# Experts' second layer of the second batch pair as a turned Strassen product

## The chip, the core and the metric

The kernel runs on one core of a Trainium2 chip. A core has engines that run their own instruction streams and wait for one another by semaphores: TensorE (PE, the matmuls, with its weight loads as PEld), VectorE (DVE), ScalarE (ACT), GpSimd (POOL) and SyncE (SP), which here issues DMA transfers. Matmul results go to PSUM, which the kernel holds as eight banks of 128 partitions x 512 numbers (fp32); everything else lies in SBUF or in DRAM. The metric is the device time of one execution, in microseconds (us). The time before is 1825.17 us, the median of three runs (1821.54 to 1825.42).

## The reference

Three stages in fp32: an attention between tokens and 32 state slots in each of 4 batches, a feed-forward layer, and a layer of 8 experts with a balanced gate P. The change is in the third.

```python
def _moe2_ref(x, w_gate, w1, w2):            # x: 2176 x 512, w1: 8 x 512 x 1024, w2: 8 x 1024 x 512
    P = np.exp(x @ w_gate - max)
    ...                                      # eight rounds of row and column scaling of P
    for e in range(E):
        h = np.maximum(x @ w1[e], 0.0)
        out += P[:, e:e + 1] * (h @ w2[e])
```

Of the 2176 rows, 2048 are the tokens of the 4 batches (512 each) and 128 the state slots.

## The kernel before

**Numbers in two parts.** An fp32 matrix is held as two fp32r parts: the high part is a cast of it (an ACT copy), the low part what is left (a subtraction). A product takes three matmuls (`mm3`, L92 to L95): high by high, high by low, low by high. So a 128x128 weight block against 512 columns is three matmuls.

**Periods of the experts' stage.** The 4 batches are worked in two pairs. For each pair (g = 0, 1), each expert e and each piece fp of 256 of its 1024 hidden rows there is one period, 64 in all: n = 0 to 31 for the first pair, n = 32 to 63 for the second. In period n the first layer of piece n is computed, and beside it the second layer of piece n - 1.

**First layer** (`products`, from L837). A Strassen form: the two batches and the two halves of the hidden rows make a 2x2 block product in 7 products of 6 matmuls (L848), 42 in place of 48. They run in three PSUM banks p1a, p1b, p1c; the results are put together by DVE adds (L856) and an ACT copy (L861). `relu_split` makes the parts of h = relu(...): hh by ACT (L828), hl by DVE (L829), for each of f = 0, 1 (half of the piece) and c = 0, 1 (batch of the pair). The forms of w1 that the products need are made in the first pair by POOL sums (L751), a cast and POOL subtractions (L754), kept in DRAM, and loaded again in the second pair (L744).

**Second layer** (`second`, L917). For each batch c and each of 4 blocks t of 128 tokens, six matmuls (two hidden halves f, three each) into one of four banks of the pool `acc`; the tokens are the rows of the result, so the gate's factor is one number for each partition, and DVE adds p times factor to the sum in SBUF (L945). That is 8 groups, 48 matmuls, in a period. In the first pair a ninth group serves the state slots, with their own first layer (`slots_rows`, `slots_turned`). The second-layer weights come from DRAM as w2r, ACT casts them (L770) and POOL makes their low part (L772).

**What sets the order.** One program order for each engine is found by a scheduler from the order in which the loop emits the pieces and from when it expects them to be ready; between engines there are only semaphores. Each PSUM bank is used again as soon as the reader of its last contents is done, so a group of matmuls waits for the eviction of the group that had its bank. The four `acc` banks go round; between two uses of one bank lie at least 18 matmuls.

Of the kernel before, what the change touches and what calls it, by code (L numbers as in the profile page):

```python
# [19 lines left out]
def attention_ffn_experts(  # L20
# [85 lines left out]
    if True:  # L106
# [5 lines left out]
        mid_ctx = ExitStack()  # L112
        mid = mid_ctx.enter_context(right("mid"))
# [526 lines left out]
        for j in range(NJ):  # L640
# [3 lines left out]
            if not more:  # L644
# [3 lines left out]
                tmp = ctx.enter_context(right("tmp", reuse_waits="tile"))  # L648
# [57 lines left out]
        moe = ctx.enter_context(left("moe", reuse_waits="tile"))  # L706
        later.append(moe)
# [4 lines left out]
        w1_raw, w1_t, w2_raw, w2_t = {}, {}, {}, {}  # L712
        dram = ctx.enter_context(tc.tile_pool(name="dram", bufs=1, space=bass.MemoryType.DRAM))
        kept = {}

        def load(n):
# [41 lines left out]
        def keep_w1(n):  # L758
# [3 lines left out]
            kept[e, fp] = [dram.tile([P, 7 * 2 * P], F32, name=f"w1{s}_{n}") for s in "hl"]  # L762
            for part, of in zip(kept[e, fp], w1_t[n]):
                nc.sync.dma_start(part, f32(of[:, 1:].rearrange("a s k c -> a (s k c)")))

        def split_w2(n):
            r = w2_raw.pop(n)
            hi = moe.tile([P, 2, DM], F32R, tag="w2h", bufs=2, name=f"w2h{n}")
            lo = moe.tile([P, 2, DM], F32R, tag="w2l", bufs=2, name=f"w2l{n}")
# [3 lines left out]
            w2_t[n] = hi, lo  # L773
# [13 lines left out]
        gm, gma, cp, cs, rs = (small[:, a:b] for a, b in ((0, 1), (1, 2), (2, 2 + E), (10, 10 + E), (18, 18 + NTT)))  # L787

# [32 lines left out]

        h_t = {}

        def relu_split(n, f, c, src, cols=S):

            hi = moe.tile([P, cols], F32R, tag=f"hh{f}{c}", bufs=1 + (c > 0), name=f"hh{n}_{f}{c}")
            lo = moe.tile([P, cols], F32R, tag=f"hl{f}{c}", bufs=1 + (c > 0), name=f"hl{n}_{f}{c}")
# [198 lines left out]
```

## Time and profile before

| what | value |
|---|---|
| median of three runs | 1825.17 us (1821.54 to 1825.42) |
| profiled execution, its own time | 1825.2 us |
| its span, first to last instruction | 1823.4 us |
| mean granted TensorE clock | 0.993 of full |
| share busy: PE, DVE, POOL, ACT | 98%, 63%, 35%, 34% |

The span has four parts: attention to about 105 us, the feed-forward layer to about 400 us, the first pair's 32 periods to about 1150 us, and the second pair's 32 periods to the end. Busy time is the time in which an engine works on an instruction. The name on the left of an arrow in a row is what is written, on the right what is read; `p` stands for the four `acc` banks. A row with "xN" covers N instructions of one kind. Matmuls are pipelined: a row gives 0.39 us for one, though the next one starts earlier.

### The profile page before, as it was taken

The numbers are of one execution on the slowest core, as the hardware profiler recorded it, in microseconds if no ns is written. First come the engines' busy times: TensorE is split into PE (matmuls) and PEld (weight loads), VectorE is DVE, ScalarE is ACT, GpSimd is POOL, SyncE is SP. The second block draws the span as 40 slices with busy tenths as digits, with TensorE's granted clock in tenths as the row PEclk, the third lists the DMA queues.
The fourth block names the chain that finished last, engine by engine and source line by source line (L and its number), as shares of the span: only waits on it lengthen the run. The fifth ranks groups of instructions, "written<-read, shape, count | busy, mean of one in ns | idle before, by whom it ended". The sixth has DMA issues, their size and how long they took to land.

```text
span 1823.4 us, 21783 instructions
## 1 busy us (share of the span) xinstructions
PE 1790.6 (98%) x8328; PEld 1477.0 (81%) x8328; DVE 1145.0 (63%) x1764; ACT 615.0 (34%) x1086; POOL 640.1 (35%) x567
## 2 busy tenths in 40 slices
PE   5899999999999999999999999999999999999999
PEld 3678888878888888888888888888888888888887
DVE  6778887556876555555655556755555555555555
ACT  6876666544332222222222222221211121122211
POOL 4356554465554444444444443211111111111110
PEclk8899999999999999999999999999999999999999
DMA  5311110005343333333333332422332233223331
GB/s 146 97 40 66 58 47 18 3 28 176 133 137 127 127 116 119 127 127 127 127 127 127 127 127 105 156 104 104 137 123 104 104 125 135 105 104 115 135 114 47
DMA packets 100684, 194.89 MB, mean 107 GB/s; under 512 B 24676, under 2 KB 57444, under 8 KB 100580
## 3 DMA queue, kind: packets, MB, share of 16 engines
q1 hardware_dynamic: 99540, 193.24, 31.2%
q8 instruction: 65, 1.06, 0.2%
q10 hardware_dynamic: 1040, 0.26, 0.1%
q14 instruction: 39, 0.32, 0.1%
HBM read 130.30 MB, written 63.18 MB: 106 GB/s over the span
## 4 chain that ended last, share of the span: by engine, by line
PE 91%; DVE 4%; ACT 2%; issue 1%; POOL 1%; DMA 0%; DVEq 0%; ACTq 0%; POOLq 0%; SPq 0%
PE p1b L848 14%; PE p L94 14%; PE p L95 14%; PE p L93 14%; PE p1a L848 10%; PE p1c L848 10%; PE p1s L900 3%; PE yps L94 2%; PE yps L93 2%; PE yps L95 2%; DVE low L186 1%; PE hps L93 1%; PE hps L95 1%; PE hps L94 1%; DVE bits L182 1%
## 5 line engine op out<-in xcount | busy, mean ns | idle before, releaser
L945 DVE SCALAR_TENSOR_TENSOR oacc<-p,pr,oacc 128x512 f32<-128x512 f32 x472 | 352.5, 747 | 196.7 <-PE p L95 188.8
L95 PE MATMUL p<-w2h,hl 128*128 128x512 f32 x1088 | 424.5, 391 | 0.0
L93 PE MATMUL p<-w2h,hh 128*128 128x512 f32 x1088 | 423.7, 389 | 0.0
L94 PE MATMUL p<-w2l,hh 128*128 128x512 f32 x1088 | 423.6, 389 | 0.0
L772 POOL TENSOR_TENSOR w2l<-w2r,w2h 128x512 fp32r<-128x512 f32 x128 | 163.9, 1301 | 601.3 <-ACT w2h L770 601.3
L754 POOL TENSOR_TENSOR w1l<-w1r,w1h 128x768 fp32r<-128x768 f32 (+1 forms) x96 | 169.8, 1795 | 250.2 <-ACT w1h L752 248.6
L828 ACT ACTIVATE hh<-p1a 128x512 fp32r<-128x512 f32 x64 | 38.3, 598 | 610.7 <-PE p1a L848 610.7
L93 PEld LDWEIGHTS p<-w2h,hh 128*128 128x128 f32 x1088 | 204.2, 188 | 42.4
L94 PEld LDWEIGHTS p<-w2l,hh 128*128 128x128 f32 x1088 | 204.2, 188 | 42.1
L95 PEld LDWEIGHTS p<-w2h,hl 128*128 128x128 f32 x1088 | 204.2, 188 | 41.4
L848 PE MATMUL p1b<-xT,w1h 128*128 128x512 f32 x768 | 237.5, 390 | 0.0
L856 DVE TENSOR_TENSOR U<-p1b,P 128x512 f32<-128x512 f32 x128 | 88.4, 691 | 196.8 <-PE p1b L848 196.8
L848 PEld LDWEIGHTS p1b<-xT,w1h 128*128 128x128 f32 x768 | 142.4, 188 | 28.0
L848 PE MATMUL p1a<-xB,w1h 128*128 128x512 f32 x512 | 158.9, 391 | 0.0
L848 PE MATMUL p1b<-xT,w1l 128*128 128x512 f32 x384 | 149.6, 390 | 0.0
L401 POOL TENSOR_TENSOR gl<-t,gh 128x512 fp32r<-128x512 f32 x64 | 86.6, 1363 | 125.9 <-ACT gh L400 124.7
L751 POOL TENSOR_TENSOR w1r<-w1r 128x256 f32<-128x256 f32 x128 | 93.7, 743 | 104.4 <-DMA w1r<-in_moe_w_dram 99.4
L828 ACT ACTIVATE hh<-P 128x512 fp32r<-128x512 f32 x64 | 40.5, 632 | 264.9 <-DVE P L856 264.9
L829 DVE SCALAR_TENSOR_TENSOR hl<-U,hh 128x512 fp32r<-128x512 f32 x128 | 122.2, 955 | 6.9 <-ACT hh L828 6.8
L848 PEld LDWEIGHTS p1a<-xB,w1h 128*128 128x128 f32 x512 | 95.8, 188 | 19.1
L856 DVE TENSOR_TENSOR U<-p1c,U 128x512 f32<-128x512 f32 x128 | 87.9, 686 | 28.7 <-PE p1c L848 28.6
L94 PE MATMUL yps<-gl,woh 128*128 128x512 f32 x256 | 100.6, 393 | 0.6 <-POOL gl L401 0.6
(199 smaller groups left out, 2933.3 us busy)
## 6 DMA issues: line engine op xcount, KB each, us to landing
w1h<-w1h SPq DMA_DIRECT2D x64, 896.0 KB, 4.3
w1l<-w1l SPq DMA_DIRECT2D x64, 896.0 KB, 5.3
w2r<-in_moe_w_dram SPq DMA_DIRECT2D x64, 512.0 KB, 4.1
w1r<-in_moe_w_dram SPq DMA_DIRECT2D x128, 128.0 KB, 4.3
raw<-in_moe_w_in_dram SPq DMA_DIRECT2D x32, 256.0 KB, 2.9
raw<-in_moe_w_out_dram SPq DMA_DIRECT2D x32, 256.0 KB, 2.6
out_dram<-oacc SPq DMA_DIRECT2D x16, 256.0 KB, 2.4
x<-in_x_dram SPq DMA_DIRECT2D x12, 256.0 KB, 4.5
```

What stands on the lines that cost most here:

```text
L93: nc.tensor.matmul(ps, whi, xhi, start=start, stop=False, **k)
L94: nc.tensor.matmul(ps, whi, xlo, start=False, stop=False, **k)
L95: nc.tensor.matmul(ps, wlo, xhi, start=False, stop=stop, **k)
L401: nc.gpsimd.tensor_tensor(out=lo, in0=g, in1=f32(hi), op=ALU.subtract)
L751: nc.gpsimd.tensor_tensor(out=r[:, out], in0=r[:, a], in1=r[:, b], op=op)
L754: nc.gpsimd.tensor_tensor(out=lo[:, c0:c1], in0=r[:, c0:c1], in1=f32(hi[:, c0:c1]), op=ALU.subtract)
L772: nc.gpsimd.tensor_tensor(out=lo[:, i], in0=r[:, i], in1=f32(hi[:, i]), op=ALU.subtract)
L828: nc.scalar.activation(hi, src, AF.Relu)
L829: nc.vector.scalar_tensor_tensor(out=lo, in0=src, scalar=0.0, in1=f32(hi), op0=ALU.max, op1=ALU.subtract)
L848: nc.tensor.matmul(t[z], w[:, slot, k, :], x[:, m, k, :], start=(first and k == i == 0), stop=(k == 1 and i == 2), skip_group_check=True,)
L856: nc.vector.tensor_tensor(out=t[name], in0=a, in1=b, op=ALU.add)
L945: nc.vector.scalar_tensor_tensor(out=o, in0=ps, scalar=w, in1=o, op0=ALU.mult, op1=ALU.add)
```

## The change

1. **Second layer of the second pair, pieces 32 to 62.** The 2x2 block product (256 hidden rows by two batches, 512 columns of the result in two halves) becomes a Strassen product of 7 products P1 to P7. The result is turned: columns of d are the partitions, and 512 tokens the free side. Each product has two halves u, each of three matmuls: 42 in place of 48. The weights stand still as 128x128 blocks of w2 or its sums; the moving side is h, or its sums T1 to T4.
2. **Sums over the pieces.** Each product keeps its own sum over the 31 pieces. P6 stays in two of the four `acc` banks for good (`IN_PLACE`); the other twelve groups of a period share the two banks left. P3, P2, P7 and P5 are added to their sums in SBUF by DVE (L1114). P1 and P4 (`BY_ACT`) have their sum copied from SBUF into the bank by ACT before the matmuls (L1102), and back by ACT after (L1112).
3. **The gate.** With tokens on the free side the factor is no longer a number for each partition. It is multiplied into h by DVE (`gated`, in place of L828 and L829), from rows that a DMA spreads over all partitions once per expert; a transpose of the gate at n = 6 makes them.
4. **Forms of h.** For each piece POOL makes the sums T3, T1, T2, T4 (`less`, L939); `form` casts seven matrices by ACT (L921) and subtracts by POOL (L922).
5. **Forms of w2.** Made in the first pair (four POOL sums, a cast, two POOL subtractions for each piece, beside what is there for the first pair's own second layer), kept in DRAM by six DMAs a period, loaded in the second pair as 1 MB (`load_w2(n, 0)`) and 768 KB (`load_w2(n - 1, 1)`, one buffer). The w2r load, its cast and its two POOL subtractions go in the second pair.
6. **The end.** Piece 63 stays as it was, but for the gate (48 matmuls, DVE adds); the seven sums are put together by 14 adds, and turned back by 32 transposes in 8 groups (L1144) and 8 ACT copies (L1145), onto which piece 63 is added.
7. **Tiles.** The tiles of the first layer's results and of h come from one ring of 18 (`k2`).

```diff
...
+        def k2(name, dtype=F32, shape=(P, S)):
+            return moe.tile(list(shape), dtype, tag="k2", bufs=18, name=name)
...
+        def sum_w2(n):
+
+            r = w2_raw[n].rearrange("p i (u d) -> p i u d", u=2)
+            r11, r12, r21, r22 = r[:, 0, 0], r[:, 1, 0], r[:, 0, 1], r[:, 1, 1]
+            for out, a, b, op in (
+                (r22, r21, r22, ALU.add), (r21, r11, r21, ALU.subtract), (r11, r22, r11, ALU.subtract),
+                (r12, r12, r11, ALU.subtract),
+            ):
+                nc.gpsimd.tensor_tensor(out=out, in0=a, in1=b, op=op)
...
+        def split_s2(n):
+
+            r = w2_raw.pop(n).rearrange("p i (u d) -> p (i u) d", u=2)
+            w2_s[n] = both = over.tile([P, 2, 4, HALF], F32R, tag="w2s", name=f"w2s{n}")
+            nc.scalar.copy(both[:, 0], r)
+            for c in (0, 2):
+                nc.gpsimd.tensor_tensor(
+                    out=both[:, 1, c:c + 2], in0=r[:, c:c + 2], in1=f32(both[:, 0, c:c + 2]), op=ALU.subtract
+                )
...
+            one = dram.tile([P, 2, 4, HALF], F32, name=f"w2a_{n}")
+            two = dram.tile([P, 2, 3, HALF], F32, name=f"w2c_{n}")
+            for z in range(2):
+                nc.sync.dma_start(one[:, z, :2], b[:, z, 0::2])
+                nc.sync.dma_start(two[:, z, :2], s[:, z, 0::3])
+            nc.sync.dma_start(one[:, :, 2:], s[:, :, 1:3])
+            nc.sync.dma_start(two[:, :, 2], b[:, :, 3])
+            kept_w2[e, fp] = [one, two]
+        def load_w2(n, i):
+
+            of = kept_w2[periods[n][1:]]
+            if i < len(of):
+                slots = of[i].shape[2]
+                w2_t[n, i] = (over if i else moe).tile(
+                    [P, 2, slots, HALF], F32R, tag="w2s" if i else "w2", bufs=1 if i else 2, name=f"w2{n}_{i}"
+                )
+                nc.sync.dma_start(f32(w2_t[n, i]), of[i])
...
+        def gated(n, f, c, src, to):
+
+            e = periods[n][1]
+            rows = gate_rows["all"][:, e % 2, c].rearrange("p t q -> p (t q)")
+            nc.vector.scalar_tensor_tensor(out=to, in0=src, scalar=0.0, in1=rows, op0=ALU.max, op1=ALU.mult)
+            raw_t[n, f, c] = to
+
+        def form(n, name, raw):
+
+            hi, lo = (k2(f"{name}{s}{n}", F32R) for s in "hl")
+            nc.scalar.copy(hi, raw)
+            nc.gpsimd.tensor_tensor(out=lo, in0=raw, in1=f32(hi), op=ALU.subtract)
+            form_t[n, name] = hi, lo
...
+            gated(n, f, c, src, own)
+            if n == END:
+                form(n, f"h{f}{c}", own)
+                h_t[n, f, c] = form_t[n, f"h{f}{c}"]
+            elif (f, c) != (0, 1):
+                form(n, f"h{f}{c}", own)
...
+        def less(out, a, b):
+            nc.gpsimd.tensor_tensor(out=out, in0=a, in1=b, op=ALU.subtract)
+
+        def h_sums(n):
+
+
+            b11, b12, b21, b22 = (raw_t[n, f, c] for f in range(2) for c in range(2))
+            t3 = t2_raw[0][:, 0]
+            return [
+                lambda: less(t3, b22, b12),
+                lambda: (form(n, "T3", t3), less(b12, b12, b11)),
+                lambda: (form(n, "T1", b12), less(b22, b22, b12)),
+                lambda: (form(n, "T2", b22), less(b21, b21, b22)),
+                lambda: form(n, "T4", b21),
+            ]
...
+            if g:
+                nc.vector.tensor_tensor(out=o, in0=ps, in1=o, op=ALU.add)
...
+        ORDER = (
+            ("P3", 0, 3, "h11"), ("P1", 0, 0, "h00"), ("P2", 0, 1, "h10"), ("P7", 0, 2, "T3"),
+            ("P5", 1, 1, "T1"), ("P6", 1, 0, "T2"), ("P4", 1, 2, "T4"),
+        )
+        FIRST = len(periods) // 2
+        IN_PLACE = ("P6",)
+        BY_ACT = ("P1", "P4")
...
+                if name in IN_PLACE:
+                    held[name] = [acc_bank(f"m{name}_{i}") for i in range(2)]
...
+        def turned_product(n, name, part, slot, what, u):
+
+            w = w2_t[n, part][:, :, slot, u * P:(u + 1) * P]
+            hi, lo = form_t[n, what]
+            m = sums_of(name, u)
+            kept, first, last = name in IN_PLACE, n == FIRST, n == END - 1
+            onto = name in BY_ACT and not first
+            ps = m if kept else acc_bank(f"p2_{n}_{name}{u}")
+            if onto:
+                nc.scalar.copy(ps, m)
+            goes_on = onto or (kept and not first)
+            for i, (a, b) in enumerate(((0, hi), (1, hi), (0, lo))):
+                nc.tensor.matmul(
+                    ps, w[:, a], b, start=(i == 0 and not goes_on), stop=(i == 2 and (last or not kept)),
+                    skip_group_check=True,
+                )
+            if kept:
+                return
+            if onto or first:
+                nc.scalar.copy(m, ps)
+            else:
+                nc.vector.tensor_tensor(out=m, in0=ps, in1=m, op=ALU.add)
...
+                [lambda u=u: add(u, "P2", "P1", "P2", nc.gpsimd) for u in range(2)],
+                [lambda u=u: add(u, "P1", "P6", "P1") for u in range(2)],
+                [lambda u=u: add(u, "P5", "P1", "P5") for u in range(2)],
+                [lambda u=u: add(u, "P3", "P5", "P3", nc.gpsimd if u else nc.vector) for u in range(2)],
+                [lambda u=u: add(u, "P1", "P1", "P7", nc.gpsimd if u else nc.vector) for u in range(2)],
+                [lambda u=u: add(u, "P7", "P5", "P7", nc.gpsimd if u else nc.vector) for u in range(2)],
+                [lambda u=u: add(u, "P4", "P1", "P4") for u in range(2)],
...
+            for k in range(KD):
+                of = held[(("P2", "P4"), ("P3", "P7"))[c][k // 2]][k % 2]
+                nc.tensor.transpose(ps[:, k * P:(k + 1) * P], of[:, t * P:(t + 1) * P], ident)
+            nc.scalar.copy(oacc[1, c][:, t, :], ps)
...
+            elif n and n <= END:
+                seconds = [
+                    lambda r=r: [turned_product(n - 1, *r, u) for u in range(2)] for r in ORDER
+                ]
...
+                        load_w2(n, 0)
+                        if n > FIRST:
+                            load_w2(n - 1, 1)
...
+            if g and n < END:
+                sums_now = h_sums(n)
+                sums_now.pop(0)()
...
+        for c in (1, 0):
+            for t in range(NT):
+                turn(c, t)
+        for c in (1, 0):
+            for t in range(NT):
+                second(END, c, t)
...
```

In a steady period of the second pair TensorE has 84 matmuls in place of 90. Its order at the last product of piece 44: P40 and P41 are the two halves of product P4, p2_45_P30 and P31 the first product of the next piece. A row is one matmul, `[waits ...]` the engines it waits for (Activation is ACT). After:

```order
L1105 MATMUL p2_44_P40_13271<-T4h44_13210,w244_1_13134 128x512 [waits Activation_49]
L1105 MATMUL p2_44_P40_13271<-T4h44_13210,w244_1_13134 128x512
L1105 MATMUL p2_44_P40_13271<-T4l44_13211,w244_1_13134 128x512 [waits Pool_49]
L1105 MATMUL p2_45_P30_13304<-h11h45_13206,w245_0_13132 128x512 [waits DMAHW4_49,Activation_49]
L1105 MATMUL p2_45_P30_13304<-h11h45_13206,w245_0_13132 128x512
L1105 MATMUL p2_45_P30_13304<-h11l45_13207,w245_0_13132 128x512
L1105 MATMUL p2_44_P41_13277<-T4h44_13210,w244_1_13134 128x512 [waits Activation_49]
L1105 MATMUL p2_44_P41_13277<-T4h44_13210,w244_1_13134 128x512
L1105 MATMUL p2_44_P41_13277<-T4l44_13211,w244_1_13134 128x512
L1105 MATMUL p2_45_P31_13309<-h11h45_13206,w245_0_13132 128x512 [waits DVE_49]
```

What moved: P3 of the next piece follows P4 at once. P30 is written into the bank of P40, and its wait for Activation is for the copy of P40 out of that bank; P31 is written into the bank of P30, once DVE has read it, with the three matmuls of P41 between. Before, at the same place of the program (the second layer of piece 46, batch 1, blocks t = 0 and 1), TensorE has:

```order
L93 MATMUL p2_46_1_0_12766<-w2h46_12543,hh46_01_12655 128x512 [waits DVE_49]
L94 MATMUL p2_46_1_0_12766<-w2l46_12544,hh46_01_12655 128x512
L95 MATMUL p2_46_1_0_12766<-w2h46_12543,hl46_01_12656 128x512
L93 MATMUL p2_46_1_0_12766<-w2h46_12543,hh46_11_12599 128x512
L94 MATMUL p2_46_1_0_12766<-w2l46_12544,hh46_11_12599 128x512
L95 MATMUL p2_46_1_0_12766<-w2h46_12543,hl46_11_12600 128x512
L93 MATMUL p2_46_1_1_12785<-w2h46_12543,hh46_01_12655 128x512 [waits DVE_49]
```

What was there: six matmuls go to a bank, and the next one waits for the read of a bank filled four groups ago. ScalarE at the same place, after (T1h, T2h are casts of h's sums; m6 is the sum of P4, m2 that of P1):

```order
L921 CAST T1h45_13322<-U2_45_13152 128x512 [waits PE_49,Pool_49]
L1102 COPY p2_44_P40_13271<-m6_11250 128x512 [waits DVE_49]
L921 CAST T2h45_13349<-U3_45_13202 128x512 [waits PE_49,Pool_49]
L1112 COPY m6_11250<-p2_44_P40_13271 128x512 [waits PE_49,Activation_49]
L1102 COPY p2_44_P41_13277<-m6_11250 128x512 [waits DVE_49]
L1112 COPY m6_11250<-p2_44_P41_13277 128x512 [waits PE_49,Activation_49]
L1102 COPY p2_45_P10_13331<-m2_11140 128x512 [waits Activation_49]
L1102 COPY p2_45_P11_13337<-m2_11140 128x512 [waits DVE_49]
```

And before, where one period of the second pair has six ACT instructions, all of the first layer or of w2:

```order
L770 CAST w2h46_12543<-w2r46_12396 128x1024 [waits DMAHW3_49,PE_49,Pool_49]
L861 COPY P1_46_12539<-p1a_46_12530 128x512 [waits DVE_49,PE_49]
L828 ACTIVATE hh46_00_12617<-p1a_46_12530 128x512 [waits PE_49]
L828 ACTIVATE hh46_11_12599<-U3_46_12596 128x512 [waits DVE_49]
L828 ACTIVATE hh46_10_12636<-P1_46_12539 128x512 [waits DVE_49]
L828 ACTIVATE hh46_01_12655<-U2_46_12562 128x512 [waits DVE_49]
L770 CAST w2h47_12688<-w2r47_12541 128x1024 [waits DMAHW6_49,PE_49,Pool_49]
```

What moved: copies into and out of the product's bank stand on ACT in turn with the casts of T1 and T2, where before ACT did no work on the `acc` banks. At the end of the program, TensorE's rows after, from P5 of piece 62 on (p2_63_1_0 is the first group of piece 63):

```order
L1105 MATMUL p2_62_P50_16263<-T1h62_16186,w262_1_16166 128x512 [waits DVE_49]
L1105 MATMUL p2_62_P50_16263<-T1h62_16186,w262_1_16166 128x512
L1105 MATMUL p2_62_P50_16263<-T1l62_16187,w262_1_16166 128x512
L1105 MATMUL p2_62_P51_16268<-T1h62_16186,w262_1_16166 128x512 [waits DVE_49]
L1105 MATMUL p2_62_P51_16268<-T1h62_16186,w262_1_16166 128x512
L1105 MATMUL p2_62_P51_16268<-T1l62_16187,w262_1_16166 128x512
L1105 MATMUL p2_62_P40_16303<-T4h62_16238,w262_1_16166 128x512 [waits Activation_49]
L1105 MATMUL p2_62_P40_16303<-T4h62_16238,w262_1_16166 128x512
L1105 MATMUL p2_62_P40_16303<-T4l62_16239,w262_1_16166 128x512 [waits Pool_49]
L93 MATMUL p2_63_1_0_16379<-w263_0_16164,h01h63_16299 128x512 [waits DMAHW0_49,DVE_49]
L94 MATMUL p2_63_1_0_16379<-w263_0_16164,h01h63_16299 128x512
L95 MATMUL p2_63_1_0_16379<-w263_0_16164,h01l63_16300 128x512 [waits Pool_49]
```

What moved: piece 63 follows P4 of piece 62 in the same two banks, and no first-layer matmuls stand between these groups any more.

## Rows read from the trace of the kernel before

**Rows 1.** The page: busy time, share of the span and instructions by engine.

```profile
PE 1790.6 (98%) x8328; PEld 1477.0 (81%) x8328; DVE 1145.0 (63%) x1764; ACT 615.0 (34%) x1086; POOL 640.1 (35%) x567
```

**Rows 2.** The page: chain that ended last, by engine.

```profile
PE 91%; DVE 4%; ACT 2%; issue 1%; POOL 1%; DMA 0%; DVEq 0%; ACTq 0%; POOLq 0%; SPq 0%
```

**Rows 3.** Stretches: start:end, length, busy time by engine, clock, DMA share, GB/s.

```profile
1399.81:1420.21 20.40, 20.40 (x92) 16.89 (x90) 11.40 (x18) 4.03 (x7) 2.54 (x2) 1.00 0.32 116
1268.00:1798.00 530.00, 530.00 (x2340) 438.87 (x2339) 296.53 (x442) 104.63 (x156) 65.91 (x52) 1.00 0.31 112
600.00:624.90 24.90, 24.90 (x118) 20.79 (x117) 14.04 (x20) 6.38 (x9) 12.00 (x12) 1.00 0.39 132
90.00:105.00 15.00, 14.41 (x88) 10.37 (x86) 8.41 (x19) 10.36 (x24) 4.65 (x4) 1.00 0.01 2
```

**Rows 4.** Chain of waits from 1780 us to the end: by line; last piece.

```profile
by line: PE p L95 20.7%; PE p L93 20.6%; PE p L94 20.6%; PE p1b L848 12.4%; PE p1c L848 9.3%; PE p1a L848 6.7%; DVE oacc L945 1.7%; issue 0.1%
...
1819.57 0.75 DVE oacc L945
```

**Rows 5.** Timeline (start, length, engine): last matmul of a bank, ACT's copy.

```profile
1401.62 0.39 PE L848 MATMUL p1a<-xB,w1l 128*128 128x512 f32 x1
...
1402.05 0.59 ACT L861 COPY P<-p1a 128x512 f32<-128x512 f32 x1 [0.26 <-PE p1a L848]
```

**Rows 6.** Timeline: last matmul of a bank, DVE's add, ACT's activation.

```profile
1418.62 0.39 PE L848 MATMUL p1c<-xB,w1l 128*128 128x512 f32 x1
...
1419.05 0.69 DVE L856 TENSOR_TENSOR U<-p1c,U 128x512 f32<-128x512 f32 x1 [0.67 <-PE p1c L848]
...
1419.77 0.63 ACT L828 ACTIVATE hh<-U 128x512 fp32r<-128x512 f32 x1 [0.73 <-DVE U L856]
```

**Rows 7.** Timeline: TensorE starts again after waiting.

```profile
124.84 1.29 DVE L386 TENSOR_TENSOR t<-hps,t 128x512 f32<-128x512 f32 x2
...
125.58 0.50 PE L93 MATMUL hps<-ath,mh 128*128 128x512 f32 x1 [0.45 <-DVE t L386]
...
125.92 0.39 PE L94 MATMUL hps<-atl,mh 128*128 128x512 f32 x1
```

**Rows 8.** Answer on L423 and L408: ns min/median/max, first and last start.

```profile
L423 ACT COPY yacc<-yps x28: 559/586/596, 141.1 to 401.5; 128x512 f32<-128x512 f32 x28
...
L408 ACT COPY yps<-yacc x28: 572/590/643, 126.9 to 390.8; 128x512 f32<-128x512 f32 x28
```

**Rows 9.** The page's costliest groups: busy, mean ns, idle before.

```profile
L945 DVE SCALAR_TENSOR_TENSOR oacc<-p,pr,oacc 128x512 f32<-128x512 f32 x472 | 352.5, 747 | 196.7 <-PE p L95 188.8
...
L772 POOL TENSOR_TENSOR w2l<-w2r,w2h 128x512 fp32r<-128x512 f32 x128 | 163.9, 1301 | 601.3 <-ACT w2h L770 601.3
...
L856 DVE TENSOR_TENSOR U<-p1b,P 128x512 f32<-128x512 f32 x128 | 88.4, 691 | 196.8 <-PE p1b L848 196.8
...
L751 POOL TENSOR_TENSOR w1r<-w1r 128x256 f32<-128x256 f32 x128 | 93.7, 743 | 104.4 <-DMA w1r<-in_moe_w_dram 99.4
```

**Rows 10.** Timeline of one period of the first pair: POOL and DVE.

```profile
909.58 0.68 DVE L829 SCALAR_TENSOR_TENSOR hl<-U,hh 128x512 fp32r<-128x512 f32 x1
...
917.07 5.35 POOL L754 TENSOR_TENSOR w1l<-w1r,w1h 128x768 fp32r<-128x768 f32 x3 [9.61 <-ACT w1h L752]
917.55 1.91 DVE L829 SCALAR_TENSOR_TENSOR hl<-U,hh 128x512 fp32r<-128x512 f32 x1 [0.18 <-ACT hh L828]
```

**Rows 11.** Timeline: a group of transposes.

```profile
108.64 0.60 PE L358 MATMUL xsps<-ident,yacc_s 128*128 128x128 f32 x4
```

**Rows 12.** DMA issues from 1268 to 1798 us: KB each, us to landing.

```profile
w1h<-w1h SPq DMA_DIRECT2D x25, 896.0 KB, 4.5
w1l<-w1l SPq DMA_DIRECT2D x25, 896.0 KB, 6.4
w2r<-in_moe_w_dram SPq DMA_DIRECT2D x25, 512.0 KB, 3.3
```

More of the change, by code (lines that the diff above doesn't have):

```diff
@@ L787, in attention_ffn_experts @@
         gm, gma, cp, cs, rs = (small[:, a:b] for a, b in ((0, 1), (1, 2), (2, 2 + E), (10, 10 + E), (18, 18 + NTT)))
+        tmp_ctx.close()
+        over = ctx.enter_context(left("over", reuse_waits="tile"))
         def emit_first():
@@ L820, in sinkhorn, with turn_gates, load_gates @@
                 yield
+        turned, gate_rows = [], {}
+        def turn_gates():
+            ps, rows = bank("prps"), k2("prt")
+            n = 2 * NT * E
+            nc.tensor.transpose(ps[:n, :P], pr.rearrange("p t e -> p (t e)")[:, n:2 * n], ident)
+            nc.scalar.copy(rows[:n, :P], ps[:n, :P])
+            turned.append(dram.tile([n, P], F32, name="prd"))
+            nc.sync.dma_start(turned[0], rows[:n, :P])
+        def load_gates(e):
+            if not gate_rows:
+                gate_rows["all"] = moe.tile([P, 2, 2, NT, P], F32, tag="w1r", name="gate_rows")
+            of = turned[0].rearrange("(c t e) q -> e c t q", c=2, e=E)[e]
+            for c in range(2):
+                nc.sync.dma_start(gate_rows["all"][:, e % 2, c], of[c].unsqueeze(0).to_broadcast([P, NT, P]))
         h_t = {}
         def relu_split(n, f, c, src, cols=S):
-            hi = moe.tile([P, cols], F32R, tag=f"hh{f}{c}", bufs=1 + (c > 0), name=f"hh{n}_{f}{c}")
-            lo = moe.tile([P, cols], F32R, tag=f"hl{f}{c}", bufs=1 + (c > 0), name=f"hl{n}_{f}{c}")
+            if cols == S:
+                hi, lo = (k2(f"h{s}{n}_{f}{c}", F32R) for s in "hl")
+            else:
+                both = k2(f"h{n}_{f}{c}", F32R)
+                hi, lo = both[:, :cols], both[:, cols:2 * cols]
             nc.scalar.activation(hi, src, AF.Relu)
@@ L903, in slots_rows @@
                     )
[L904 removed]
+            h_t[n, "rows"] = k2(f"p1s_{n}")[:, :2 * P]
             nc.scalar.activation(h_t[n, "rows"], ps[:, :2 * P], AF.Relu)
@@ new lines, in attention_ffn_experts, with sums_of @@
+        FIRST = len(periods) // 2
+        IN_PLACE = ("P6",)
+        BY_ACT = ("P1", "P4")
+        def sums_of(name, u):
+            if name not in held:
+                if name in IN_PLACE:
+                    held[name] = [acc_bank(f"m{name}_{i}") for i in range(2)]
+                else:
+                    k = len([z for z in held if z not in IN_PLACE and isinstance(z, str)])
+                    if k % 2 == 0:
+                        held[k] = big.tile([P, 4, S], F32, tag="y", bufs=B, name=f"m{k}")
+                        held["tile"] = held[k]
+                    held[name] = [held["tile"][:, 2 * (k % 2) + i] for i in range(2)]
+            return held[name][u]
@@ new lines, in together, with add @@
+        def together():
+            m = held
+            def add(u, to, a, b, on=nc.vector):
+                on.tensor_tensor(out=m[to][u], in0=m[a][u], in1=m[b][u], op=ALU.add)
+            return [
+                [lambda u=u: add(u, "P2", "P1", "P2", nc.gpsimd) for u in range(2)],
[6 more added lines that the diff above has]
+            ]
@@ new lines, in turn @@
+        def turn(c, t):
+            if (1, c) not in oacc:
+                oacc[1, c] = (
+                    big.tile([P, NT, DM], F32, tag="y", bufs=B, name=f"oacc1_{c}") if c == 0
+                    else moe.tile([P, NT, DM], F32, tag="w1h", bufs=2, name=f"oacc1_{c}")
+                )
+            ps = bank(f"ct{c}_{t}")
+            for k in range(KD):
+                of = held[(("P2", "P4"), ("P3", "P7"))[c][k // 2]][k % 2]
+                nc.tensor.transpose(ps[:, k * P:(k + 1) * P], of[:, t * P:(t + 1) * P], ident)
+            nc.scalar.copy(oacc[1, c][:, t, :], ps)
@@ L990, in attention_ffn_experts @@
                     seconds[i]()
-                if n < len(periods) and periods[n][0] == 0:
+                if n < len(periods) and g == 0:
                     if i == 5:
```

115 lines of the change are left out of this document (74 added, 41 removed).

## Prediction, made before the changed kernel was run

> **What bounds the kernel now.** I read busy times first, then the stretches, then the chain of waits. TensorE is busy 98% of the span [rows 1] and holds 91% of the chain that ended last [rows 2]. In the second pair it does not stop at all: 530.00 us busy of 530.00, 2340 matmuls at a granted clock of 1.00 (2.4 GHz), so 530/2340 = 0.2265 us for each, and a period of 90 is 20.40 us, which one period shows alike [rows 3]. In the chain from 1780 us on, TensorE's three second-layer lines and three first-layer groups make up all but 1.8%, and one DVE add of 0.75 us ends it [rows 4]. So a matmul removed in the second pair is worth 0.2265 us, and any wait that TensorE meets there costs its full length. The other engines have room: in the 20.40 us DVE is busy 11.40, ACT 4.03, POOL 2.54 [rows 3].
>
> **What goes.** 31 pieces x 6 matmuls = 186, by 0.2265: -42.1 us. This is certain, as TensorE has no idle time there to absorb it.
>
> **What comes on TensorE.** 32 transposes at the end and one for the gate. Four took 0.60 us [rows 11], 0.15 each: +5.0 us.
>
> **The wait at P4, twice a period.** Today each second-layer group finds its bank free, since 18 or more matmuls lie between two uses. After, the order puts P30 of the next piece right behind P40, in the same bank, and its wait is for ACT's copy of P40 out of it. The last matmul of a bank starts at 1401.62 and ACT's copy of the result at 1402.05: 0.43 us [rows 5]. The copy takes 0.59, the same as the 586 ns of a PSUM-to-SBUF copy in the feed-forward layer [rows 5, 8]. From its end to the waiting matmul about 0.05: two DVE adds take 1.29 us from 124.84, one alone 0.69, so the first ended near 125.53, and TensorE started at 125.58 [rows 7, 9]. Without the wait P30 would start 0.23 after P40's last matmul. Idle: 0.43 + 0.59 + 0.05 - 0.23 = 0.84 us. A start after a wait costs more: the second matmul came at 125.92, 0.34 after the first and not 0.23 [rows 7], +0.11.
>
> P31 then waits until DVE has read P30; only P41's three matmuls lie between. From the start of P30's last matmul: 0.43 to DVE's start (1418.62 to 1419.05), 0.69 for the add [rows 6], 0.05 for the hop, less 4 x 0.2265 = 0.91: 0.26 us, and 0.11 for the restart.
>
> Together 0.84 + 0.11 + 0.26 + 0.11 = 1.32 us a period. The order has this pattern 29 times (pieces 33 to 61): +38.3 us. A steady period is then 84 x 0.2265 + 1.32 = 20.35 us, as long as before. The bounds: nothing, if the copy were not in the way (below), and 2.2 us if P41 too waits for its copy in, which comes behind P40's copy out on ACT: 0.43 + 0.59 + 0.59 + 0.05 = 1.66 after P40's last start, against 0.43 + 0.59 + 0.05 + 0.68 = 1.75, when P30's three matmuls are through; so P41 just makes it, and I take 1.32. The clock I leave at 1.00: it was 1.00 where TensorE was busy 14.41 of 15.00 us [rows 3], 96%, and 19.03 of 20.35 would be 94%. Behind P40's copy out on ACT stand the copy in for P41 and those for P1; these have P31 and six T4 matmuls of the first layer to hide behind (2.0 us), and are not late by these numbers.
>
> **The other engines in the second pair.** ACT has 16 instructions a period (7 casts, 8 copies, P1), for 6: some 16 x 0.6 = 9.6 us of 20.35. DVE keeps 17: 5 adds at 0.69, 4 gate products and 8 evictions which I take at L945's 0.75 [rows 9], 12.5 us. Neither is full. POOL goes from 2 to 11 instructions of 128x512: by L772's 1.30 [rows 9], 14.3 us. They form a loop: T2's low part frees the tile that the next U3 add writes, and T3 cannot begin before the next U2 and U3 are there. I add to 14.3 what POOL has to wait in that loop, three DVE steps and two ACT steps, 3 x 0.69 + 2 x 0.63 + 0.75 = 4.1 [rows 6, 9], and 1.2 for one conflict with DVE (next), and get 19.6: under 20.35, with 0.7 to spare. So POOL costs nothing while TensorE loses its 1.32 us, and would hold the period at about 19.6 if that loss were gone.
>
> The conflict: beside three POOL subtractions in SBUF, a DVE operation with two SBUF inputs took 1.91 us in place of 0.68 [rows 10], 1.23 more; I count it once a period, since three of the four gate products (on U3, P1, U2) read two SBUF tiles, and bound it by 0 and by 3 x 1.23 = 3.7 us. The Trainium skill ("SBUF — State Buffer", section "SBUF: two separate sides") says why: DVE with two SBUF inputs and a GpSimd operation that reads SBUF hold one pair of ports as an exclusive lock, and whoever comes second is fully blocked. By that rule all three gate products could be blocked in every period, it speaks against sums of h on POOL, and the sum would be rival B's; the trace agrees that one of them can be.
>
> **DMA.** In the second pair 0.5 MB of w2r a period becomes 1.75 MB, so 3.5 MB for 2.3 and a share near 0.31 x 3.5/2.3 = 0.47 [rows 3, 12]. The 768 KB part has one buffer: it is issued when P41 has read the last, and P6 wants it 27 matmuls later, 6.1 us; the nearest rows are 3.3 us for 512 KB and 4.5 for 896 KB [rows 12], so it comes in time. w1h is issued about 23 matmuls ahead of its first use, 5.2 us, for 4.5 us today: 0.7 to spare. I take 0, with 0.5 us a period as the upper bound.
>
> **First pair.** TensorE keeps its 110 instructions a period in nearly the same order. POOL gets four subtractions of 128x256 (0.74) and two of 128x512 (1.30) more, 5.6 us on 12.0 of 24.90 [rows 3, 9]; ACT one cast, SP six stores. These lie beside full TensorE work and nothing in the order waits for them before the next period, so 0; if a lock delays an eviction by 0.06 us a period the price is 2 us, and I keep 0 to 2.
>
> **The end.** Without first-layer work the 62nd piece runs through two banks: five groups wait as P31 does, 5 x 0.37 = 1.9; P40's copy in after P51 costs 0.43 + 0.69 + 0.59 + 2 x 0.05 - 0.23 - 0.68 = 0.9 and a restart, 1.0; the first transposes wait for one DVE add more, about 1.1. I take +4.0, between 1 and 8 (all 14 adds and 8 copies partly open). The last eviction and the output stay as they are.
>
> **Sum.** 1825.2 (the profiled execution, which is the median of the runs to 0.03) - 42.1 + 5.0 + 38.3 + 4.0 = 1830.4: I say 1830 us. What the measurement can tell from no change is 0.2%, 3.65 us, so 1821.5 to 1828.8 is "same".
>
> **Rivals.**
> A. *The copy hides.* P30 does not wait as the order says, because the hop and copy are shorter when ACT is ready, or the restart is free and P31 fits. For it: nothing but that the waits in other parts of the program are small. Against: a bank cannot be filled before it is read, and 0.43 + 0.59 are measured. With half the wait 1825.2 - 42.1 + 5.0 + 19.2 + 4.0 = 1811; with none the POOL loop's 19.6 holds the period, (19.6 - 19.03) x 29 = 16.5, near 1809; without that too, 1792. Chance 0.20.
> B. *POOL and DVE become the bound* (slower). The loop of 19.6 becomes the period where a second and third lock add more than 0.7 us: with two more, 22.1 us, +1.7 x 29 = 49, 1880; with one more, 20.8, +14, 1844. For it: the 1.91 us row, and 11 POOL instructions in line. Against: the locks need both to start within the same 0.7 us. Chance 0.10, at about 1850.
> C. *w1h or the second part of w2 lands late* (slower). It decides from 0.7 us more on w1h's landing: at half a microsecond past that in each of 29 periods, +14.5, 1845. For it: the share rises by half, and w1l already takes 6.4 us behind w1h [rows 12]. Against: the share stays under a half. Chance 0.12.
> D. *No change.* The restart's 0.11 us does not come twice a period, and the rest is as said: -6.4 us, 1824. Chance 0.16.
>
> **How the numbers follow.** My forecast's own case has 0.42, and lies between 1826 and 1838; a quarter of it (0.11) falls under 1828.8. Slower: 0.31 + 0.10 + 0.12 = 0.53; same: 0.11 + 0.16 = 0.27; faster: A, 0.20. The range from 1808 to 1850 leaves out about 0.10 of A (both waits gone and POOL free) and 0.08 of B and C.
>
> **What would show it.** In a steady period TensorE's first matmul of P30 idle behind ACT's copy L1112 for about 0.95 us, P31 behind DVE's L1114 for 0.3, 29 times, and no other wait of TensorE over 0.1 us; period 20.35 us; POOL near 14.3 us busy of it with 11 instructions; clock 1.00. A period of 19.0 us with no wait on L1112 would make the prediction wrong by 38 us, a wait of first-layer T4 or P4 matmuls on DVE or POOL would say B, one on DMA C.

## The result, and the profile after

The changed kernel takes 1839.53 us (median of 4 runs, 1838.15 to 1840.24), the kernel before 1824.51 in the same comparison: ratio 1.0084, 95% interval 1.0067 to 1.0102. So it is slower by some 15 us, where 1830 us was forecast, in a range of 1808 to 1850. Times are medians of executions in the fast state; one execution of a later kernel (the one whose forms are not stored) took 2904.92 us at a granted clock of 0.578, is left out of its time, and is the only traced one of that kernel. The profiled execution's span is 1837.8 us, 14.4 more than before.

The page's first lines (busy time by engine, then the chain that ended last by engine), which answer to [rows 1, 2]:

```profile
PE 1773.8 (97%) x8175; PEld 1438.3 (78%) x8175; DVE 1189.4 (65%) x1765; ACT 816.2 (44%) x1440; POOL 1211.1 (66%) x1045
...
PE 82%; DVE 7%; ACT 4%; POOL 3%; issue 2%; DMA 2%; SPq 0%; POOLq 0%; ACTq 0%; DVEq 0%
```

TensorE has less to do and is idle for longer. Where, the stretches show (columns as in [rows 3]; one steady period, the steady part of the second pair, a period of the first pair):

```profile
1399.77:1420.20 20.43, 19.61 (x85) 15.61 (x84) 12.03 (x17) 9.31 (x16) 14.82 (x12) 1.00 0.72 207
1268.00:1790.00 522.00, 500.68 (x2137) 395.91 (x2136) 306.11 (x435) 239.37 (x410) 375.08 (x278) 1.00 0.53 183
600.00:624.90 24.90, 24.90 (x118) 20.76 (x117) 14.81 (x19) 7.44 (x10) 17.45 (x17) 1.00 0.62 205
```

A period of 84 matmuls takes 20.43 us, as long as one of 90 did [rows 3]. In the first pair TensorE stays full, though POOL works 17.45 us in place of 12.00. Between 1250 and 1790 us the table of TensorE's waits (total, times, longest) has one row. It counts only idle time of over 0.15 us behind the modelled end of a matmul, so shorter waits are not in it. In the chain of waits from 1240 to 1790 us ACT's copy appears by line:

```profile
PE p_P L1105 <- ACT m L1112: 19.7, 27, 0.7
```

```profile
by line: PE p_P L1105 36.2%; PE p1b L965 20.1%; PE p1a L965 13.5%; PE p1c L965 13.1%; PE mP L1105 6.4%; DVE m L1114 3.4%; ACT T2h L921 3.1%; ACT m L1112 2.9%; issue 1.0%; ACTq L921 0.1%; ACTq L1112 0.1%
```

The timeline of the place itself, in one period (T4 matmuls are P4, h11 those of P3; weight loads left out, other rows at the dots):

```profile
1412.94 0.62 ACT L921 CAST T2h<-U 128x512 fp32r<-128x512 f32 x1 [0.78 <-PE p_P L1105]
1413.14 0.39 PE L1105 MATMUL p_P<-T4l,w 128*128 128x512 f32 x1
1413.62 0.58 ACT L1112 COPY m<-p_P 128x512 f32<-128x512 f32 x1
1414.11 0.60 ACT L1102 COPY p_P<-m 128x512 f32<-128x512 f32 x1
...
1414.26 0.73 PE L1105 MATMUL p_P<-h11h,w 128*128 128x512 f32 x2 [0.73 <-ACT m L1112]
1414.83 0.40 PE L1105 MATMUL p_P<-h11l,w 128*128 128x512 f32 x1
...
1415.27 0.69 DVE L1114 TENSOR_TENSOR m<-p_P,m 128x512 f32<-128x512 f32 x1 [1.69 <-PE p_P L1105]
1415.53 0.40 PE L1105 MATMUL p_P<-T4l,w 128*128 128x512 f32 x1
...
1416.01 0.73 PE L1105 MATMUL p_P<-h11h,w 128*128 128x512 f32 x2
```

P40's last matmul starts at 1413.14, ACT copies the bank out from 1413.62 (behind the cast of T2, which ends 0.05 before), P30 starts at 1414.26: 1.12 us from start to start in place of 0.23. P31 starts 0.48 after P41's last, behind DVE's read of P30. At each restart the second matmul comes 0.34 us after the first, 0.11 more than in the steady stream. Over the 27 periods of that stretch the start-to-start times of the h11 matmuls exceed 0.2265 us by 37.0 us in all, 1.37 a period.

Outside the steady periods, TensorE's waits in the first pair up to period 9 and at the change of pairs; before, it had no such row in either:

```profile
PE p L93 <- ACT hh L903: 2.0, 2, 1.8
PE p L95 <- DVE hl L904: 0.6, 1, 0.6
...
PE p L93 <- ACT hh L903: 0.8, 1, 0.8
PE p L93 <- DVE oacc L1067: 0.2, 1, 0.2
```

The 14.4 us, by start-to-start times of TensorE over 0.2265 us against before: removed matmuls -42.1; transposes +3.5; first pair +3.2; change of pairs +1.7, and +1.2 at one place in the fourth period behind it; the P4 place in 29 periods +40; steps of 0.230 to 0.238 us in the second pair, which were 0.2265 before, +2.3; the end +4.2. These make 14.0; the rest is in smaller steps.

### The profile page after: what moved, and what is told of

Its sections match the earlier page's. It is cut to its first block, busy times and chain, and to the rows that moved or that the text cites. A ratio compares the mean times of both kernels' runs of the same rounds, so it can differ in the third digit from the quotient of the medians.

```text
span 1837.8 us, 23228 instructions
## 1 busy us (share of the span) xinstructions
PE 1773.8 (97%) x8175; PEld 1438.3 (78%) x8175; DVE 1189.4 (65%) x1765; ACT 816.2 (44%) x1440; POOL 1211.1 (66%) x1045
## 4 chain that ended last, share of the span: by engine, by line
PE 82%; DVE 7%; ACT 4%; POOL 3%; issue 2%; DMA 2%; SPq 0%; POOLq 0%; ACTq 0%; DVEq 0%
PE p1b L965 13%; PE p_P L1105 12%; PE p1a L965 9%; PE p1c L965 9%; PE p L93 7%; PE p L95 7%; PE p L94 6%; PE yps L93 2%; PE yps L94 2%; PE yps L95 2%; PE mP L1105 2%; PE p1s L1017 2%; DVE low L187 1%; DVE m L1114 1%; ACT T2h L921 1%
## 5 line engine op out<-in xcount | busy, mean ns | idle before, releaser
L1114 DVE TENSOR_TENSOR m<-p_P,m 128x512 f32<-128x512 f32 x240 | 164.4, 687 | 174.1 <-PE p_P L1105 174.1
L1067 DVE SCALAR_TENSOR_TENSOR oacc<-p,pr,oacc 128x512 f32<-128x512 f32 x224 | 166.2, 744 | 111.7 <-PE p L95 111.6
L93 PE MATMUL p<-w2b,hh 128*128 128x512 f32 x512 | 199.9, 390 | 2.9 <-ACT hh L903 2.7
L94 PE MATMUL p<-w2b,hh 128*128 128x512 f32 x512 | 199.3, 389 | 0.0
L95 PE MATMUL p<-w2b,hl 128*128 128x512 f32 x512 | 197.0, 390 | 0.6 <-DVE hl L904 0.6
L922 POOL TENSOR_TENSOR h11l<-U,h11h 128x512 fp32r<-128x512 f32 x32 | 55.0, 1718 | 132.3 <-ACT h11h L921 132.3
L793 ACT CAST w2s<-w2r 128x1024 fp32r<-128x1024 f32 x32 | 33.7, 1053 | 229.9 <-POOL w2r L787 229.9
L1102 ACT COPY p_P<-m 128x512 f32<-128x512 f32 x120 | 71.1, 592 | 110.9 <-DVE m L1114 109.6
L904 DVE SCALAR_TENSOR_TENSOR hl<-U,hh 128x512 fp32r<-128x512 f32 x64 | 100.0, 1562 | 29.4 <-ACT hh L903 29.4
L93 PEld LDWEIGHTS p<-w2b,hh 128*128 128x128 f32 x512 | 96.1, 188 | 24.2 <-ACT hh L903 3.7
L95 PEld LDWEIGHTS p<-w2b,hl 128*128 128x128 f32 x512 | 96.1, 188 | 21.1 <-DVE hl L904 1.3
L94 PEld LDWEIGHTS p<-w2b,hh 128*128 128x128 f32 x512 | 96.1, 188 | 19.7
L965 PEld LDWEIGHTS p1a<-xB,w1h 128*128 128x128 f32 x512 | 92.8, 188 | 19.6 <-issue 2.1
```

Source lines behind the costliest of these rows:

```text
L93: nc.tensor.matmul(ps, whi, xhi, start=start, stop=False, **k)
L94: nc.tensor.matmul(ps, whi, xlo, start=False, stop=False, **k)
L95: nc.tensor.matmul(ps, wlo, xhi, start=False, stop=stop, **k)
L904: nc.vector.scalar_tensor_tensor(out=lo, in0=src, scalar=0.0, in1=f32(hi), op0=ALU.max, op1=ALU.subtract)
L965: nc.tensor.matmul(t[z], w[:, slot, k, :], x[:, m, k, :], start=(first and k == i == 0), stop=(k == 1 and i == 2), skip_group_check=True,)
L1067: nc.vector.scalar_tensor_tensor(out=o, in0=ps, scalar=w, in1=o, op0=ALU.mult, op1=ALU.add)
```

## Experiments

Theories: (1) P30 and P31 wait for a bank because two banks serve twelve groups, and this eats the removed matmuls; (2) POOL and DVE limit the second pair; (3) w1h, the high part of the first layer's weights, comes late; (4) the loss is made in the first pair and at the end. The ratios are to the kernel before (medians 1822 to 1824 us).

**Four banks.**

```diff
-        IN_PLACE = ("P6",)
+        IN_PLACE = ()
```

> The product P6 no longer stays in two acc banks; DVE adds it to a sum in SBUF as it does P3, so 14 groups share four banks. P30 then follows P40 by 9 or more matmuls and in another bank. Theory (two banks: the waits of P30 and P31, 1.42 us a period, eat the 186 matmuls): TensorE has no wait on ACT's L1112 any more; the period falls from 20.45 us to 19.0 if nothing else limits, and the time to about 1839.5 - 29 x 1.42 = 1798 us; with POOL's loop at 19.6 us a period about 1815. Rival (POOL and DVE in their loop limit the second pair, the wait on ACT only shows where they end): period stays at or over 20.2 us and TensorE's waits move to DVE or POOL, time 1833 or more. Second rival (the time is lost in the first pair and at the end, outside the steady periods): 1836 or more.

Measured: 1809.91 us, 0.9929 (0.9915 to 0.9943). No wait on L1112 is left, so theory (1) holds for the bank, and 30 us come back; but not all. TensorE's waits between 1260 and 1740 us are now on transfers:

```profile
PE p1a L965 <- DMA w1h<-w1h: 8.5, 4, 3.1
PE p1a L965 <- DMA w1l<-w1l: 0.9, 2, 0.6
```

The timeline of one such place: the rows of the gate are issued 0.47 us ahead of w1h in the same queue.

```profile
1386.97 0.37 SPq L892 DMA_DIRECT2D gate_rows<-prd  x1
...
1387.44 0.46 SPq L748 DMA_DIRECT2D w1h<-w1h  x1
...
1395.61 0.62 PE L965 MATMUL p1a<-xB,w1h 128*128 128x512 f32 x1 [2.16 <-DMA w1h<-w1h]
```

w1h lands 8.1 us after issue, 4.3 to 4.8 in the periods without gate rows ahead of it. And TensorE is granted half its clock behind that wait:

```profile
1391.50:1395.60 4.10, 1.95 (x9) 1.29 (x7) 2.48 (x4) 2.00 (x4) 4.02 (x4) 1.00 0.99 381
1395.60:1399.40 3.80, 3.79 (x10) 2.96 (x11) 0.69 (x1) 0.71 (x2) 2.42 (x3) 0.55 0.91 299
```

So it was behind two of the four waits (2.2 and 3.1 us). Behind another, of 2.1 us, the granted clock stayed at 1.00 (1557 to 1561 us).

**P4 by DVE, still two banks.**

```diff
-        BY_ACT = ("P1", "P4")
+        BY_ACT = ("P1",)
```

> P4 is added to its sum by DVE and no longer copied into the bank and out of it by ACT; P6 still holds two banks. The order then is P40, P41, P30, then six first-layer matmuls, then P31: P41 and P30 each wait for DVE with three matmuls between. Theory (a bank cannot be filled before it is read, so each such place costs 0.26 + 0.11 = 0.37 us): 2 x 0.37 = 0.74 us a period in place of 1.42, period 19.8 us, time 1839.5 - 29 x 0.68 = 1820 us. Rival (it is ACT's copy in and out alone): no wait left, period 19.0, 1798 us. Rival (POOL's loop limits): period over 20.2 us, 1833 or more.

Measured: 1817.59 us, 0.9965 (0.995 to 0.998), a period of 19.72 us (433.93 us in 22 periods), 0.70 over 84 matmuls. Expected were 0.74 and 1820. P41 waits as said; P30 hardly does (0.24 us from start to start), since P41's own delay covers it (weight loads left out at first, other rows at the dots):

```profile
1404.91 0.39 PE L1105 MATMUL p_P<-T4l,w 128*128 128x512 f32 x1
1405.41 0.73 PE L1105 MATMUL p_P<-T4h,w 128*128 128x512 f32 x2
...
1405.97 0.40 PE L1105 MATMUL p_P<-T4l,w 128*128 128x512 f32 x1
...
1406.21 0.63 PE L1105 MATMUL p_P<-h11h,w 128*128 128x512 f32 x2
...
1406.68 0.40 PE L1105 MATMUL p_P<-h11l,w 128*128 128x512 f32 x1
...
1406.92 0.30 PEld L965 LDWEIGHTS p1b<-xT,w1h 128*128 128x128 f32 x2 [0.28 <-DVE U L973]
1406.92 0.73 PE L965 MATMUL p1b<-xT,w1h 128*128 128x512 f32 x2
```

So the price of a bank used again after three matmuls, with DVE as its reader, is what the rows of before gave (0.50 - 0.23 + 0.11 = 0.38 here). It is paid once a period and not twice as expected. That the sum came near 0.74 all the same is luck: some 0.12 of the 0.70 is a second slow step in each period, at the first layer's bank p1b behind DVE's add of U, and the rest lies in short waits on w1h and steps a little over 0.2265 us.

**Four banks, no ACT copies.**

```diff
-        IN_PLACE = ("P6",)
-        BY_ACT = ("P1", "P4")
+        IN_PLACE = ()
+        BY_ACT = ()
```

> Both edits and more: P6 not in place, and P1 and P4 added by DVE too, so DVE has 14 evictions a period and ACT none. Theory: as with four banks alone, no bank wait; DVE goes to 23 operations, about 16.5 us of the period, still under it; 1798 to 1815 us, equal to the kernel with four banks and ACT copies within 5 us. If ACT's 8 copies were themselves a limit, it would be faster than that one by more than 5 us; if DVE were near its limit, slower by more than 5 us.

Measured: 1795.01 us, 0.9848 (0.9835 to 0.9862): faster than both kernels. TensorE is full for 22 periods, 19.17 us each:

```profile
1308.24:1729.89 421.65, 421.13 (x1857) 348.15 (x1856) 331.48 (x509) 102.05 (x177) 307.00 (x242) 1.00 0.55 199
```

POOL's 307.00 us are 14.0 a period, as forecast, and it holds nobody up: theory (2) falls, and so does the loop of 19.6 us. That it is 15 us faster than with ACT's copies was not expected, and at first read as a cost of the copies. The next run speaks against that.

**Four banks with ACT's copies, without most gate rows.**

```diff
-                    if fp == 0:
+                    if fp == 0 and e < 2:
                         load_gates(e)
```

> Four banks with ACT's copies (1810 us, while the version without ACT's copies takes 1795), and the gate rows of experts 2 to 7 of the second pair are not loaded (the rows of the first two experts are used for all: the second pair's output is not the reference's). Theory: the 15 us between the two versions are w1h's transfer, which in every fourth period is issued behind a 256 KB broadcast of gate rows and lands after 8.0 to 8.1 us in place of 4.5, so that TensorE waits for it (8.5 us in all), and is granted half its clock after a wait of 2.2 us. Then every w1h lands in 4.5 us, no period is over 20 us, and the time is 1795 us. Rival (ACT's copies in and out of the banks are slow in themselves): the slow periods stay, 1806 us or more. Rival (w1h is late because the share of the DMA engines is over a half anyway): half of it, 1802.

Measured: 1792.78 us, 0.9836 (0.9823 to 0.9848). Its row of stretches has no idle time, at full clock, with the copies still there (ACT 199.05 us):

```profile
1309.34:1728.65 419.31, 419.31 (x1851) 347.19 (x1850) 281.79 (x421) 199.05 (x352) 320.98 (x242) 1.00 0.54 193
```

This kernel is 17 us faster than the one with all gate rows. So the 15 us were w1h behind the gate rows: theory (3) in a form that was not forecast, in one period of four. In the changed kernel the order issues w1 first, and w1h lands in 4.2 to 4.7 us throughout.

**Gate rows held back.** In the version without ACT copies, a one-column ACT copy into the rows keeps their load behind w1's.

```diff
+                if after is not None:
+                    nc.scalar.copy(gate_rows["all"][:, e % 2, c, 0, :1], after[:, :1])
                 nc.sync.dma_start(gate_rows["all"][:, e % 2, c], of[c].unsqueeze(0).to_broadcast([P, NT, P]))
...
+            if g and periods[n if n <= END else END][2] == 1 and FIRST + 4 < n < END - 4:
+                load_gates(periods[n][1] + 1, raw_t[n, 0, 1])
```

> Four banks and no ACT copies (1795 us), and each load of gate rows is held back by a one-column ACT copy until the second period of an expert, behind w1's loads in SyncE's queue. Theory (gate rows ahead of w1h delay it to 8.6 to 10 us): w1h lands in 6.5 us or less in every period, no period over 20 us, and 2 to 3 us less, 1792 us. Rival (without ACT's copies w1h has time enough even at 10 us, only the order changes): 1795 us, within 1 us.

Measured: 1795.56 us, 0.9843 (0.983 to 0.9856), no gain: the rival. The longest landing of w1h fell from 10.0 us to 7.8, but the version without ACT copies had had only 0.5 us of wait on it: where gate rows stood ahead of w1h, its first user came 9.5 us after its issue, with ACT's copies at the place above 5.9. A late transfer costs where its first user stands close, not by itself.

**The first pair alone.** The second pair as before, w2's forms made and stored but not read (classical `second`, `relu_split` and loads of w2r in all periods; the edit is long, its core is)

```diff
-            elif n and n <= END:
-                seconds = [
-                    lambda r=r: [turned_product(n - 1, *r, u) for u in range(2)] for r in ORDER
-                ]
...
-                    else:
-                        load_w2(n, 0)
...
+                    load(n + 1)
+                    split_w2(n)
```

> The first pair's part alone: w2's Strassen forms are made and stored to DRAM in the first pair as in the changed kernel, but never read; the second pair is worked as before (48 matmuls, w2 loaded, cast and split again, gate's factor in the eviction). Theory: this part costs the 3.0 us by which the changed kernel is late at period 9, so the time is before + 3 us (0.15%), in two waits of TensorE in the first eight periods. Rival (it costs nothing by itself, the 3 us come from the gate's turning and the order): before within 1 us. Rival (DVE's operations blocked by POOL's sums cost in each period): before + 5 us or more.

Measured: 1828.91 us, 1.0037 (1.0023 to 1.0051), +6.7 us, between 4.2 and 9.3. More than the 3 expected. Its trace has both waits of the changed kernel, in the first periods and at the change of pairs: from period 0 to 9 it takes 204.8 us for 201.8 before, and 1.7 more by period 33.

```profile
PE p L93 <- ACT hh L905: 2.2, 2, 1.5
PE p L95 <- DVE hl L906: 0.6, 1, 0.6
PE p L93 <- DVE oacc L1069: 0.2, 1, 0.2
```

**Two buffers for the raw w2.** 

```diff
-            return moe.tile(list(shape), dtype, tag="k2", bufs=18, name=name)
+            return moe.tile(list(shape), dtype, tag="k2", bufs=16, name=name)
...
-            w2_raw[n] = moe.tile([P, 2, DM], F32, tag="w2r", name=f"w2r{n}")
+            w2_raw[n] = moe.tile([P, 2, DM], F32, tag="w2r", bufs=2, name=f"w2r{n}")
```

> The first pair's part alone again, with two buffers for the raw w2 in place of one (and 16 tiles in the ring in place of 18, to make room). Theory: in the first periods the raw w2 is held until the last POOL subtraction of its forms, its next load comes late, the cast of it stands on ACT ahead of h's activations, and TensorE waits for these (1.9 and 1.3 us). With two buffers the load is early: from period 0 to 9 the kernel takes 201.8 us as before, not 204.8, and the time is before + 1.5 to 3 us in place of + 6.6. Rival (POOL is simply full in the first periods, or DVE's operations are blocked by it): no change in the first periods, before + 6 us.

> Four banks, no ACT copies, and two buffers for the raw w2 with a ring of 16 tiles. Theory: as for the first pair alone, 3 us less than the version with one buffer, so 1792 us; the ring of 16 costs nothing, since TensorE had no wait on it. Rival (the ring of 18 was needed in the second pair, where h, its sums and its forms all live in it): waits of TensorE or POOL for tiles, 1800 us or more. Rival (the buffer is not the cause): 1795.

Measured: for the first pair alone 1830.84 us, 1.0044 (1.0031 to 1.0057), no better, and 207.0 us from period 0 to 9. With four banks and no ACT copies 1818.67 us, 0.9975 (0.9965 to 0.9986), 24 us worse than with the ring of 18. A second buffer paid for with two tiles of the ring gains nothing. The theory of the held buffer is not decided by this, since the ring became smaller in the same edit: in the first pair the wait for ACT's hh in the first periods (1.5 us with one buffer) is gone, and 2.9 us of waits on DVE have come. In the second pair with 16 tiles, w1h is again waited for; why was not settled:

```profile
PE p1a L965 <- DMA w1h<-w1h: 15.3, 7, 3.8
```

**What in the first pair costs.** The forms without their stores, and the forms from period 6 on:

```diff
-                if i == 5 and g == 0:
-                    keep_w2(n)
```

```diff
-                if i == 2 and g == 0:
+                if i == 2 and g == 0 and n >= 6:
                     sum_w2(n)
```

(and the same condition for `split_s2` and `keep_w2`)

> The first pair's part alone, with w2's forms made on POOL and ACT but not stored to DRAM (the second pair works as before and doesn't need them). If POOL's and ACT's work for the forms costs the 6.6 us: before + 5 us or more, as with the stores. If the six stores a period cost it (SyncE's queue and the DMA engines): before + 1 us or less.

> The first pair's part alone, but w2's forms are made and stored only from period 6 on (those of the first six periods are left out; the second pair doesn't need them here). Theory (the cost lies in the first periods, where POOL and DVE also balance the gate, and at the change of pairs): period 9 is reached after 201.8 us as before, and before + 1.5 to 2.5 us is left from the change of pairs. Rival (a cost in each period): before + 4 us or more.

Measured: without stores 1828.5 us, 1.0023 (1.0014 to 1.0032), +4.2 us (2.6 to 5.8), between the two cases and not clear of the kernel with stores; from period 6 on 1825.97 us, 1.0008 (0.9999 to 1.0017), +1.5 us, with 201.7 us from period 0 to 9, as before. So the first pair's cost lies in its first six periods and at the change of pairs, not in the 26 periods between, and the engines' work for the forms makes it at least in part. From period 9 to 31 the first-pair kernel takes 516.85 us, as before. Which of that work is the late one was not settled, nor whether the stores add to it. Theory (4) holds for a smaller part: some 5 us in the first pair and at the change of pairs, and the 4 at the end that were forecast.

## Why the prediction was right, and where it was short

The direction, the mechanism and the place were right; the size was 5 us forecast for 15 measured, so a third of it.

- *What goes* (-42.1): held. 84 matmuls and no waits make 19.06 us a period in the version without most gate rows (419.31 us in 22 periods), for 84 x 0.2265 = 19.03.
- *The wait at P4* (+38.3): held, 1.37 us a period for 1.32, with P30 at 1.12 from P40's last (1.07 forecast) and P31 at 0.48 (0.48 forecast: 0.26 + 0.23). Four banks remove it; with DVE in place of ACT 0.38 is left at this place. The 0.05 is the cast of T2 ahead of the copy, which stood in ACT's order and had no price in the sum.
- *Rival D* falls: the restart is paid twice a period, 0.34 us for the second matmul both times.
- *First pair* (0 to 2): the step that failed. It (3.2 us) and the change of pairs (1.7), for which there was no term, cost 4.9 us in the trace and 4.2 to 9.3 by the run with the first pair alone. "Nothing in the order waits for them before the next period" held in the steady periods, not in the first six.
- *The end* (+4.0): 4.2. *Transposes* (+5.0): 3.5, at some 0.11 us from one to the next; 0.15 counted the length of the last one four times.
- *Not forecast*: 2.3 us in steps of 0.230 to 0.238 us in the second pair, and 1.2 in its fourth period, at two waits for DVE's gate product and for w1l.
- *Rival B*: POOL's time a period was right (14 us) and its loop wrong. 19.6 added the DVE and ACT steps as if POOL stood idle in all of them; it overlaps them with other pieces' subtractions. The conflict exists: of the gate products on U half take 0.68 us and half about 1.6 (mean 1136 ns below), and POOL's two subtractions beside them take 1.75 us, not 1.30:

```profile
L915 DVE SCALAR_TENSOR_TENSOR U<-U,gate_rows 128x512 f32<-128x512 f32 x53 | 60.2, 1136 | 0.9
L922 POOL TENSOR_TENSOR h11l<-U,h11h 128x512 fp32r<-128x512 f32 x27 | 47.6, 1761 | 102.1 <-ACT h11h L921 102.1
L922 POOL TENSOR_TENSOR h00l<-t_raw,h00h 128x512 fp32r<-128x512 f32 x26 | 45.3, 1741 | 0.0
...
1420.92 1.29 POOL L922 TENSOR_TENSOR T4l<-P,T4h 128x512 fp32r<-128x512 f32 x1
...
1421.13 1.64 DVE L915 SCALAR_TENSOR_TENSOR U<-U,gate_rows 128x512 f32<-128x512 f32 x1
...
1422.17 1.73 POOL L922 TENSOR_TENSOR h00l<-t_raw,h00h 128x512 fp32r<-128x512 f32 x1
```

  The Trainium skill ("SBUF — State Buffer", section "SBUF: two separate sides") has one engine of the two fully blocked. The trace agrees: the slow gate product starts 0.21 us into T4's subtraction, which keeps its 1.29 us, and ends 0.56 us after it; the next subtraction, issued 0.60 us before the product's end, is the late one then, by 0.43. The 0.96 us that the product loses are within the forecast's bound of 1.23. In the version with four banks and no ACT copies, where the operations fall otherwise, the same rows show 717 and 1311 ns. TensorE waits for none of it.
- *Rival C*: w1h had its 4.4 us (median) in the changed kernel, and was not late, but by luck: its first user came 4.79 us after its issue in most periods, not 5.2, and the longest landing was 4.74, so some 0.05 us were to spare and not 0.7. It was late in the version with four banks, where the gate rows stood ahead of it in the queue. The mean share of the DMA engines was 0.54 there, and 0.54 too without the gate rows, where it was not late; in the first 5 us behind the issue (1386.50 to 1391.50) the share was 0.30.

## What to carry to other kernels

A product with fewer matmuls can save nothing, as here, if it halves the PSUM banks that the others share: count, for each bank, the matmuls between two uses, and compare them with the last matmul's lead (0.43 us), the reader (0.59 or 0.69) and the restart. Where a sum is kept in place in PSUM to spare an eviction, try the plain eviction first: here DVE had the room. Four banks turned +15 us into -13, and with P1 and P4 left to DVE too it was -28. After each such step look again at what TensorE waits for: the next wait (w1h behind the gate rows) was not in the profile before.

## What the runs showed of the hardware

- A matmul that restarts after a wait of some 0.3 to 0.9 us is followed after 0.34 us, not 0.23, and steps of 0.230 to 0.238 us follow; the granted clock stays at 1.00. The wait itself need not be long: with P4 by DVE, 0.34 us follow a p1b matmul that came 0.24 us after the one before. There and at P30 the first weight load starts together with its matmul (1406.92 us there, 1414.26 in the changed kernel); whether that is the cause was not tried.
- After a wait of 2.2 us in a stretch with 1.95 us busy of 4.10, the granted clock fell to 0.55 for the next 3.8 us (1.2 GHz for nearly all of it): 10 matmuls where 0.2265 us each would be 2.3 us, so 1.5 us lost beside the wait. It did not follow every such wait: after one of 2.1 us the clock stayed at 1.00.
- A 256 KB transfer that spreads rows of 512 bytes over all partitions, issued just ahead of an 896 KB one, moved that one's landing from 4.5 to 8.1 us.
- A DVE operation that reads two SBUF tiles took 1.64 us for 0.68 where a POOL subtraction was running when it began, and the POOL subtraction behind it 1.73 for 1.30. One that reads a PSUM bank and one tile took 0.69 beside POOL.
